# Linear attention and a gated feed-forward block on one core: the first batch's loads, the rule for PSUM banks and the order of group 0's output tiles

One NeuronCore of a Trainium2 chip runs the whole program. The metric is device time in microseconds (us), the median of several executions; all comparisons use executions in the fast state. "Span" is the time from the first to the last instruction of the one profiled execution, some 2 us less than the device time.

## The reference, cut

```python
B, H, S, D = 8, 8, 576, 64
def phi(x, c, s):
    r = np.maximum(x, 0.0)
    return np.concatenate([r * c, r * s], axis=-1)      # c, s: cos and sin of pi/2 * position / S
q_p, k_p = phi(q, cos_w, sin_w), phi(k, cos_w, sin_w)
kv  = np.einsum('bhsf,bhsd->bhfd', k_p, v)
num = np.einsum('bhsf,bhfd->bhsd', q_p, kv)
den = np.einsum('bhsf,bhf->bhs', q_p, np.sum(k_p, axis=2))[..., None] + 1e-06
x   = (num / den).transpose(0, 2, 1, 3).reshape(4608, 512)
out = (silu(x @ w_gate) * (x @ w_val)) @ w_out          # w_gate, w_val 512 x 1536, w_out 1536 x 512
```

## The kernel before

The 4608 rows go through the feed-forward part (FFN) in nine groups of 512. The attention of a batch is worked into the FFN of the group before it by a plan: `at(slot, step)` puts a step behind the products of a slot; a group has 16 slots. Loads with a cast (fp32 to bf16) are issued by GpSimd and share one queue; what needs no cast, the output writes and the DMA transposes ("turns") are issued by SyncE and share another.

```python
raw = ctx.enter_context(tc.tile_pool(name="raw", bufs=3))     # k, v, q of three batches at a time
...
def take(n, hold=None):                                       # PSUM banks in ring order, those held left out
    while True:
        b0 = (bank_at[0] + n - 1) // n * n % 8
        bank_at[0] = b0 + n
        if not any(b0 <= x < b0 + n for r in held.values() for x in r):
            break
...
def load(b, nm, parts=1):                                     # casting load, GpSimd
    ...
        nc.gpsimd.dma_start(out=t[:, sl].rearrange("p g c d -> p g (c d)"), in_=sv[:, sl])
def qturn_dma(b, e):                                          # turn of q by DMA, SyncE
    nc.sync.dma_start_transpose(out=qt_of(b)[:, e]..., in_=st[b, "q"][e * SH:(e + 1) * SH]...)
def qturn_pe(b, j, lo, hi, eng):                              # the same by PE and an engine that reads PSUM
    ...
def a_half(t, j):                                             # numerators of 128 rows: reads qt and kvd
    ...
for piece in range(3):                                        # group 0's output: four tiles side by side
    for t in range(OUT):
        ffn_out(t, 4 * piece, 4 * piece + 4)
        slot((piece, t))
for b in range(2, B):
    s0 = SLOTS * (b - 1)
    ...
        if b > 3:
            for s, nm in ((p0 - 2, "k"), (p0, "v"), (p0 + 2, "q")):
                at(s, lambda b=b, nm=nm: load(b, nm))         # waits until batch b-3 has left its buffers
    for e in range(2):
        at(tq[e], lambda b=b, e=e: qturn_dma(b, e))
```

## Time and profile before

| | before |
|---|---|
| device time | 339.96 us (339.66 to 344.24) |
| span | 337.0 us |
| PE busy | 97% of it |
| first FFN product | 18.23 us |
| first product of group 0's output | 45.11 us |
| first product of group 1 | 61.55 us |

The last three rows cut the span into an opening, group 0's FFN, group 0's output with batch 1's attention worked in, and the rest.

### The profile page before, as it was taken

How to read it: one execution, taken by the hardware profiler on the slowest of the kernel's cores; microseconds unless marked ns; L12 is line 12 of the kernel's file. 1: busy time of each engine (PE TensorE's matmuls, PEld its weight loads, DVE VectorE, ACT ScalarE, POOL GpSimd, SP SyncE). 2: the span in 40 equal slices, each digit the busy share in tenths (PEclk: the TensorE clock that was granted, in tenths of full speed). 3: DMA queues.
4: the chain of work that ended last, by engine and by line, in shares of the span. 5: the costliest groups of instructions: out<-in, count | busy, mean ns of one | idle time of the engine just before them, and what ended most of it. 6: DMA issues, size and time to landing. Idle time of an engine off the chain costs nothing.

```text
span 337.0 us, 5960 instructions
## 1 busy us (share of the span) xinstructions
PE 325.9 (97%) x2280; PEld 167.6 (50%) x2313; DVE 189.0 (56%) x424; ACT 158.0 (47%) x311; POOL 32.4 (10%) x50
## 2 busy tenths in 40 slices
PE   8889998999999999999999999999999999999995
PEld 3578854454444444444454444544454444444443
DVE  6664756389526952695259625971478138714420
ACT  6664456778326732673257415751354135413321
POOL 9454320011002000200000000000000000000000
PEclk9999999999999999999999999999999999999999
DMA  8999999999976828492810271017301410141013
GB/s 238 198 200 200 204 207 208 252 185 186 159 150 100 147 58 168 72 168 48 160 27 17 48 153 45 16 31 143 71 17 31 104 38 16 34 109 31 0 33 93
DMA packets 57084, 36.76 MB, mean 109 GB/s; under 512 B 31328, under 2 KB 52064, under 8 KB 57056
## 3 DMA queue, kind: packets, MB, share of 16 engines
q0 software_dynamic: 20624, 18.03, 33.8%
q1 hardware_dynamic: 36272, 18.23, 25.9%
q8 instruction: 18, 0.29, 0.3%
q10 hardware_dynamic: 160, 0.13, 0.1%
q14 instruction: 10, 0.08, 0.1%
HBM read 37.75 MB, written 9.44 MB: 140 GB/s over the span
## 4 chain that ended last, share of the span: by engine, by line
PE 93%; ACT 3%; DVE 2%; issue 1%; ACTq 0%
PE banks L377 53%; PE banks L403 27%; PE banks L316 5%; PE banks L132 3%; PE banks L237 3%; ACT sg L385 1%; DVE v L202 1%; DVE ht L387 1%; PE banks L357 1%; PE banks L421 0%; PE banks L285 0%; ACT xT L358 0%; PE banks L223 0%; ACT ob L410 0%; ACT qwT L277 0%
## 5 line engine op out<-in xcount | busy, mean ns | idle before, releaser
L377 PE MATMUL banks<-xT,wg_sb 128*128 128x512 bf16 (+2 forms) x474 | 112.4, 354 | 1.8 <-ACT xT L358 1.0
L387 DVE TENSOR_TENSOR ht<-sg,banks 128x512 bf16<-128x512 bf16 (+2 forms) x122 | 76.1, 624 | 66.4 <-PE banks L377 50.9
L377 PE MATMUL banks<-xT,wv_sb 128*128 128x512 bf16 (+2 forms) x479 | 111.7, 354 | 0.2
L385 ACT ACTIVATE sg<-banks 128x512 bf16<-128x512 f32 (+2 forms) x122 | 66.9, 548 | 90.3 <-PE banks L377 89.4
L403 PE MATMUL banks<-wo_sb,ht 128*128 128x512 bf16 x410 | 93.3, 379 | 0.6 <-issue 0.2
L377 PEld LDWEIGHTS <-wv_sb 128*128 128x128 bf16 x488 | 47.3, 98 | 46.3
L377 PEld LDWEIGHTS <-wg_sb 128*128 128x128 bf16 x488 | 45.8, 98 | 37.1 <-issue 2.2
L403 PEld LDWEIGHTS <-ht 128*128 128x128 bf16 x420 | 40.7, 98 | 46.1 <-issue 0.6
L410 DVE COPY ob<-banks 128x512 f32<-128x512 f32 x17 | 11.8, 692 | 56.3 <-PE banks L403 56.2
L326 ACT ACTIVATE tmp<-banks,cst 128x260 f32<-128x260 f32 x64 | 30.5, 477 | 13.6 <-PE banks L316 12.8
L410 ACT COPY ob<-banks 128x512 f32<-128x512 f32 x18 | 10.6, 587 | 55.9 <-PE banks L403 55.9
L327 DVE SCALAR_TENSOR_TENSOR num<-banks,cst,tmp 128x260 f32<-128x260 f32 x64 | 31.0, 485 | 7.1 <-ACT tmp L326 6.7
L316 PE MATMUL banks<-kvd,qt 128*128 128x260 bf16 (+1 forms) x144 | 24.9, 277 | 0.1
L341 DVE TENSOR_TENSOR x<-num,rec 128x256 bf16<-128x256 f32 x64 | 24.4, 422 | 1.1
L202 DVE TENSOR_TENSOR v<-raw_v,tab 128x1152 bf16<-128x1152 bf16 x30 | 22.3, 752 | 0.0
L316 PEld LDWEIGHTS <-qt 128*128 128x128 bf16 (+1 forms) x144 | 11.8, 100 | 16.0 <-issue 3.4
L188 ACT ACTIVATE raw_k<-raw_k 128x576 bf16<-128x576 bf16 x24 | 16.0, 675 | 0.0
L188 ACT ACTIVATE r_q<-raw_q 128x576 bf16<-128x576 bf16 x24 | 16.0, 675 | 0.0
L93 POOL DMA_DIRECT2D raw_k<-in_k_dram x9 | 7.0, 780 | 82.1 <-issue 78.9
L237 PE MATMUL banks<-v,raw_k 64*64 64x130 bf16 x576 | 11.9, 220 | 1.1 <-ACT kvd L249 0.9
L237 PEld LDWEIGHTS <-raw_k 64*64 64x64 bf16 x576 | 9.2, 106 | 7.0 <-issue 5.6
L132 PE MATMUL banks<-zeros 128*128 128x512 bf16 x37 | 11.1, 458 | 1.0 <-DVE zeros L127 1.0
(57 smaller groups left out, 113.0 us busy)
## 6 DMA issues: line engine op xcount, KB each, us to landing
out_dram<-ob SPq DMA_DIRECT2D x70, 128.0 KB, 2.4
raw_k<-in_k_dram POOLq DMA_DIRECT2D x7, 576.0 KB, 12.5
raw_v<-in_v_dram POOLq DMA_DIRECT2D x6, 576.0 KB, 13.6
raw_q<-in_q_dram POOLq DMA_DIRECT2D x6, 576.0 KB, 15.6
wg_sb<-in_moe_w_gate_dram POOLq DMA_DIRECT2D x6, 256.0 KB, 11.3
wv_sb<-in_moe_w_val_dram POOLq DMA_DIRECT2D x6, 256.0 KB, 11.3
wo_sb<-in_moe_w_out_dram POOLq DMA_DIRECT2D x3, 512.0 KB, 13.3
first_v<-in_v_dram SPq DMA_DIRECT2D x2, 576.0 KB, 4.2
```

The lines of the kernel that those rows point to most:

```text
L188: nc.scalar.activation(out=out, in_=in_, func=AF.Relu)
L202: nc.vector.tensor_tensor(out=v2s[b % 2][:, g, :, :, 0:D], in0=(first if b == 0 and g < 2 else {"v": raw_of(b, "v")})["v"][:, g].unsqueeze ...
L237: nc.tensor.matmul(out=ps[i * D:(i + 1) * D, e, j * 2 * D1:(j + 1) * 2 * D1], lhsT=raws[b, "k"][es, g, c], rhs=v2s[b % 2][es, g, c, :, 0:D ...
L316: nc.tensor.matmul(out=ps[ms, e, 0:4 * D1], lhsT=st[b, "qt"][:, e, j, c:c + n].rearrange("p c s -> p (c s)"), rhs=kvd[b % 2][:, e, j].rear ...
L326: nc.scalar.activation(out=tmp, in_=av[:, :, 0], func=AF.Copy, scale=cst[:, c0, 0:1])
L327: nc.vector.scalar_tensor_tensor(out=st["num", t][:, j], in0=av[:, :, 1], scalar=cst[:, c0, 1:2], in1=tmp, op0=ALU.mult, op1=ALU.add,)
L341: nc.vector.tensor_tensor(out=x[:, 4 * j * D:(4 * j + 4) * D].rearrange("p (i e d) -> p e i d", i=2, e=2), in0=num[:, hs, 0:D].rearrange(" ...
L377: nc.tensor.matmul(out=o, lhsT=w[:, kc, fs], rhs=xT[tg][:, kc, ts], start=(kc == 0), stop=(kc == KC - 1))
L385: nc.scalar.activation(out=sg[:, 0:n], in_=ps[0], func=AF.Silu)
L387: nc.vector.tensor_tensor(out=ht[:, fc, r:r + n], in0=sg[:, 0:n], in1=ps[1], op=ALU.mult)
L403: nc.tensor.matmul(out=o_ps[t], lhsT=ht[:, fc, r:r + P], rhs=wo_sb[:, fc], start=(fc == 0), stop=(fc == FC - 1))
L410: (nc.scalar.copy if t % 2 == 0 else nc.vector.tensor_copy)(out=ob, in_=ps)
```

## The change

Its intent has two parts. **The opening:** k and q of the first batch come in fp32 by SyncE's queue, which needs no cast; they are put where w_out and the second half of ht will stand later. q is turned first and multiplied by cos and sin afterwards, so 16 transposes do for 32. GpSimd's first weight load waits for v's second quarter (a small copy). **Group 0's output:** a bank is given by longest out of use and not in ring order, and the output tiles are worked by pairs, so two banks are held and not four.

```diff
     def take(n, hold=None):
-        while True:
-            b0 = (bank_at[0] + n - 1) // n * n % 8
-            bank_at[0] = b0 + n
-            if not any(b0 <= x < b0 + n for r in held.values() for x in r):
-                break
+        free = [b for b in range(0, 8, n) if not any(b <= x < b + n for r in held.values() for x in r)]
+        b0 = min(free, key=lambda b: sorted(used[b:b + n], reverse=True))
...
+    for gs in (slice(0, 1), slice(1, 2), slice(2, 4)):
         load_first("v", gs)
-    load_first("q", slice(0, G), slice(0, CUT[0]))
...
-    load(0, "k", 2)
-    load_slots(0, "q", CUT[0], NC)
+    load_first("k", slice(0, 1))
+    load_first("k", slice(1, 2))
+    load_first("q", slice(0, G), 0, 2)
+    load_first("k", slice(2, 3))
+    load_first("k", slice(3, 4))
+    load_first("q", slice(0, G), 2, 4)
...
+    hold = consts.tile([P, 1], FP32)
+    nc.gpsimd.tensor_copy(out=hold, in_=first["v"][:, 1, 0, 0:1])
+    load_w(0)
+    load_slots(0, "q", CUT[0], NC)
...
+    def weight_q(t):
+        for w in range(2):
+            nc.vector.tensor_tensor(out=qwT[t % 2][:, w]..., in0=qr[t % 2]..., in1=tabq[:, w, 2 * t:2 * t + 2]..., op=ALU.mult)
...
-    for piece in range(3):
-        for t in range(OUT):
-            ffn_out(t, 4 * piece, 4 * piece + 4)
-            slot((piece, t))
+    steps0 = [(piece, t) for piece in range(3) for t in range(2)] + [(piece, t) for t in (2, 3) for piece in range(3)]
+    for i, (piece, t) in enumerate(steps0):
+        ffn_out(t, 4 * piece, 4 * piece + 4)
+        slot(divmod(i, 4))
```

Cut: the opening's new order of steps (relu of k, kv, turns, first FFN products), the layout of xT, ht in two tiles. After group 0 the program is the same.

## The prediction

> **What bounds the kernel now.** I read the page first, then PE's waits over the whole span, then the chain in order of time, then the timeline of the first 30 us and of 36 to 62 us.
>
> ```profile
> PE 325.9 (97%) x2280; PEld 167.6 (50%) x2313; DVE 189.0 (56%) x424; ACT 158.0 (47%) x311; POOL 32.4 (10%) x50
> ```
>
> TensorE is the bound, and no other engine is near it. But busy time counts overlapping ends and the products on zeros (L132), so I ask where PE does no useful work. The waits of PE are few:
>
> ```profile
> PE banks L357 <- ACT ob L410: 1.3, 2, 0.7
> PE banks L132 <- DVE zeros L127: 1.0, 1, 1.0
> PE banks L377 <- ACT xT L358: 1.0, 2, 0.7
> PE banks L237 <- ACT kvd L249: 0.9, 1, 0.9
> PE banks L285 <- ACT qwT L277: 0.7, 1, 0.7
> PE banks L223 <- DVE num L327: 0.3, 1, 0.3
> ```
>
> All lie before 61 us: the same view from 62 us on is empty. Three are in the opening's chain (kvd, qwT, xT). Two are bank waits at the end of group 0 (L357 and L223 get a PSUM bank that another engine has only now stopped reading).
>
> **After 61.3 us nothing is to be had.** In the chain 16 products of 512 columns take 3.45 us, so 0.2156 us each. Eight groups of 144 make 248.4 us; 28 tiles of numerators at two times 0.22 us, with three tiles split between batches, 12.9; twelve kv halves of 0.65 us 7.8. Sum 269.1 us. PE's last product ends at 332.2, 270.9 us after 61.3, so at most 1.8 us are lost there. The 4.8 us tail (two ACT copies, output DMA) is untouched.
>
> **Before 61.3 us** I count useful PE work the same way: group 0's FFN products 96 x 4 x 0.0547 = 21.0 and 48 x 0.2156 = 10.4; transposes of weighted q 32 x 0.058 = 1.9; kv of two batches 2.6; a_tile 32 x 0.058 = 1.9; turns of x 1.8; turns of raw q 1.2; numerators 2.0. Sum 42.8 us. So some 17.5 us go to filler and waits: 8.6 before the first useful product, 5.7 from 9.4 to 24.6 us (15.2 us of time, 9.5 of work), about 1 from there to 45.1, and 2.5 from 45.1 to 61.3 (16.2 of time, 13.7 of work). The opening's chain:
>
> ```profile
> 0.99 8.61 PE banks L132 x28
> ...
> 10.08 0.72 PE banks L237 x35
> ...
> 12.67 0.85 PE banks L237 x36
> ...
> 14.49 0.48 PE banks L285 x8
> ...
> 17.75 0.64 PE banks L285 x8
> 18.39 0.91 PE banks L377 x16
> ```
>
> The first FFN product begins at about 18.2 us, and PE is filled with FFN from 24.6 us on. The two clean bank waits in the timeline:
>
> ```profile
> 57.69 0.38 PE L357 MATMUL banks<-ident,x 128*128 128x128 bf16 x4 [0.68 <-ACT ob L410]
> ...
> 60.47 0.38 PE L357 MATMUL banks<-ident,x 128*128 128x128 bf16 x4 [0.67 <-ACT ob L410]
> ```
>
> Each costs about 0.8 us of start-to-start time against an unbroken stream (the products before end their slots at 56.85 and 59.64).
>
> The arrivals of the first batch, from what began when its data landed:
>
> ```profile
> 8.34 1.71 ACT L265 ACTIVATE qw<-first_q,csk 128x256 bf16<-128x256 f32 x4 [1.11 <-DMA first_q<-in_q_dram]
> ...
> 11.01 0.46 DVE L190 TENSOR_SCALAR raw_k<-raw_k 128x1152 bf16<-128x1152 bf16 x1 [0.50 <-DMA raw_k<-in_k_dram]
> ...
> 18.82 0.74 POOL L176 DMA_DIRECT2D wg_sb<-in_moe_w_gate_dram  x1 [1.16 <-DMA wv_sb<-in_moe_w_val_dram]
> ```
>
> v landed at 4.5 and 6.0 us, the first slots of q at 8.3, k at 9.6 and 11.0. The POOL queue's waits tell when weights land: the first pair of weight slices at 15.6, the second at 18.8, the third at 21.2.
>
> **What the Trainium skill says.** "TensorE: Matmul & The Clock Gate", Part 1, gives N/2.4 GHz plus 2.5 ns for a warm product, half speed until PE has been busy for about 3.4 us, and a floor near 25 ns. The trace agrees on the first: 0.2156 us for 512 columns. The zero products' weight loads are 0.43 us apart until 6.0 us, half that after, so the slow phase was 5 us here. "DMA: Bandwidth & Descriptors", Queues, rings and completion order, says each engine goes round the queues packet by packet. Here q's first slots (0.52 MB) needed 2.36 us beside the casting k load, 222 GB/s, where v ahead of it ran at about 390. "VectorE: DVE Perf Modes", The perf-mode tier table, bears on the new products of turned q: 16-bit operands at two elements a cycle. The trace has 1152 such outputs in 0.75 us (L202), against 1.36 us from fp32. "ScalarE: Activation LUTs", What ACT_TABLE_LOAD costs, has 1283 ns a load; so has the trace, twice, and the change keeps both loads.
>
> **The change, part by part.**
>
> *First batch by the uncast queue.* In fp32 k is 1.18 MB, and q's first four slots 0.52, so 2.88 MB with v instead of 1.70. By the trace data runs from about 2.2 us at 390 GB/s and is seen 0.8 us after it has moved. Alone the queue would finish at about 10.4 us. But the weights start once v's second quarter is there (4.5 us), and in the trace a POOL load takes two us or so to move bytes, so from 6.5 us they share. Estimates: v at 3.8, 4.5 and 6.0; k's first half by 7.6; q's two slots at 8.5 to 9; k's last quarter at 10.7 with 270 GB/s for this queue or 11.6 with 222, say 11.1. That is no earlier than now. The gain must come from what follows.
>
> *q weighted after turning.* 32 transposes become 16 (the last two tiles use pairs of halves, which run side by side like L223): 0.9 us less PE. Two zero products per half of kv give back 0.4. Per tile: ACT now has four scaled relus or so and copies of 0.5 to 0.6, then one relu of 0.59; DVE has two products of about 0.4 each (512 outputs, from 0.75 for 1152).
>
> *The opening in order.* kv_first(0) starts when ACT has cast three quarters of v (5.3 to 7.2) and relu'd two of k (to 8.6). Filler ends near 8.2 to 9.3, depending on whether a 64-column zero product takes 30 or 56 ns, so I put the first useful product at 8.7, against 9.4. The last k lands at 11.1, its relus end at 11.5, kv_first(1) ends at 12.4, kvd is copied at 13.0 and a_tile(0) ends at 13.3, against 14.97. Denominator, reciprocal, two halves of x (0.17 + 0.20 + 0.42 + 0.42), turns and two parallel copies: xT is whole near 15.5, and FFN starts there, not at 18.2.
>
> From there DVE's order decides: each tile needs 1.06 for x, 0.8 for the weighting, 0.57 for two ht. a_tile(1) at 16.8, a_tile(2) at 20.0 (the second pair of weights, needed at 17.6, still lands at about 18.5, and PE waits in a gap that it had anyway), a_tile(3) at 23.1, full flow at 23.6. By then the same FFN work is done as now at 24.6 (64 short products against 32 short and 16 long, both 3.5 us), but one turn of x more remains (0.2). Gain: **0.8 us**. FFN starting 2.7 us earlier is mostly spent again in waits for DVE.
>
> *Banks and output tiles by pairs.* Before, four output banks are held through all of group 0's output, and ring order hands the turns of x a bank just left. Now two are held, and the longest unused one is given. Of the 2.5 us lost from 45.1 to 61.3 the two ob waits (1.6) should go, and the wait for num with the load after it (0.4): **2.0 us**. After 61.3: 0.2 of the 1.8, as PE's waits list nothing there.
>
> *Others.* The new layout of xT only cuts the moving operand into runs of 128, and the split ht changes addresses: 0.
>
> Sum: 0.8 + 2.0 + 0.2 = 3.0 us, and 0.5 for the fewer transposes and freer order of FFN halves behind the opening, where about 1 us was lost: 3.5 us. 339.96 - 3.5 = **336.5 us**.
>
> **Rivals.** (1) *The weights' transfers hold up k and q.* If sharing begins earlier or takes more than half, the last k lands at 12.5 and the opening gains nothing or loses 0.5: about 337.8. For it speaks 222 GB/s in the shared stretch; against it, that the weights' packets are shorter than k's, so a turn by packets favours k. (2) *The opening gains in full.* If DVE keeps up, PE's work from a_tile(0) on is some 6.7 us, so full flow could come at 20.5: 3 us more, about 333.5. Against it speaks DVE's sum of about 8 us over the same stretch. (3) *The clock.* Short zero products may fail to hold or win the full clock; the opening's products then take twice as long, costing 1 to 2 us: about 338. (4) *The bank wait is replaced.* With ob read later or x late on DVE, the turns of x wait for x itself; then the last stretch gains 0.8 and not 2.0: 337.7.
>
> **Range and chances.** The two gains are independent: the opening from -0.5 to +3, the banks from 0.8 to 2.4. That gives 334.3 to 338.8 for eight in ten. 2% is 6.8 us: it needs both in full and most of the first filler too, so 0.05. Slower by 2% would need a stall in every group, which the emptiness of PE's later waits makes unlikely: 0.01.
>
> **What would show it.** Right: no wait of PE for ob in group 0's output, that stretch near 14 us; first FFN product at 15 to 16 us; a_tile waits put down to DVE's weighting; after group 0 the same length to within 0.5 us. Wrong: k's last relu after 12 us (rival 1); weight loads of zero products 0.43 us apart beyond 6.5 us (rival 3); full FFN flow before 22 us (rival 2); any PE wait for banks after 62 us.

## More of the kernel before

Batch 2's q is the first that is turned by DMA and not by PE.

The prediction shows the waits of PE. Here are lines that it does not show, and that matter later. First the SyncE timeline of the kernel before, from 60 us (start, length, engine, operation): the turn of batch 2's q.

```profile
66.11 6.83 SPq L214 DMA_TRANSPOSE qt<-r_q  x2
```

Then GpSimd's timeline: the three casting loads of batch 5, issued once batch 2's buffers are free.

```profile
53.95 0.74 POOL L93 DMA_DIRECT2D raw_q<-in_q_dram  x1 [7.14 <-PE banks L223]
74.97 0.76 POOL L93 DMA_DIRECT2D raw_k<-in_k_dram  x1 [20.28 <-issue]
75.72 0.75 POOL L93 DMA_DIRECT2D raw_v<-in_v_dram  x1
76.45 0.76 POOL L93 DMA_DIRECT2D raw_q<-in_q_dram  x1
```

And the weight-load side of PE, where the first uses of that turned q stand, one for each of the two turns. The bracket is idle time and what ended it.

```profile
77.11 0.10 PEld L316 LDWEIGHTS <-qt 128*128 128x128 bf16 x1
77.42 0.10 PEld L316 LDWEIGHTS <-qt 128*128 128x128 bf16 x1 [0.21 <-DMA qt<-r_q]
```

The turned q comes just in time: the second turn is 0.21 us late for its weight load, and not at all late for PE's products, so that the view of PE's waits is empty here. The table by stage says how full the queues are at that time (the last two columns are the DMA engines' share, over 1 when several packets of an engine overlap in the record, and GB/s).

```profile
68.00:72.00 4.00, 3.95 (x52) 2.04 (x52) 4.00 (x7) 3.17 (x6) 0.00 (x0) 1.00 1.21 209
72.00:76.00 4.00, 3.95 (x52) 2.04 (x52) 3.12 (x7) 2.80 (x6) 1.03 (x2) 1.00 1.36 152
76.00:80.00 4.00, 4.00 (x22) 1.95 (x21) 3.90 (x10) 3.59 (x8) 1.21 (x2) 1.00 1.13 167
80.00:84.00 4.00, 4.00 (x22) 1.98 (x21) 3.90 (x11) 3.18 (x7) 0.00 (x0) 1.00 1.20 200
```

## The result

| | before | after |
|---|---|---|
| device time, median | 339.81 us (338.96 to 344.24) | 351.35 us (350.7 to 351.77) |
| span | 337.0 | 348.6 |
| first FFN product | 18.23 | 15.50 |
| first product of group 0's output | 45.11 | 45.61 |
| first product of group 1 | 61.55 | 60.01 |
| from there to the end | 275.5 | 288.6 |

The changed kernel is **slower**: ratio 1.0347, 95% interval 1.0318 to 1.0375. A ratio here is the mean time of one kernel's fast runs over that of the other's of the same rounds, so not quite the ratio of the medians quoted. (The run of 344.24 is more than 1.5% above the fastest, so it counts as slow and is left out of the ratio.)

The waits of PE, all of them, in the changed kernel (total us, times, longest):

```profile
PE banks L375 <- DMA qt<-r_q: 10.9, 2, 7.4
PE banks L296 <- ACT raw_k L214: 1.5, 2, 1.2
PE banks L440 <- DMA wv_sb<-in_moe_w_val_dram: 1.4, 2, 0.9
PE banks L149 <- DVE zeros L144: 1.0, 1, 1.0
PE banks L440 <- DMA wg_sb<-in_moe_w_gate_dram: 0.9, 1, 0.9
```

The waits for ob and num are gone, as intended. In their place stands one that the kernel before did not have: PE waits 10.9 us for batch 2's turned q. PE's timeline puts it in group 1:

```profile
79.40 0.28 PE L375 MATMUL banks<-kvd,qt 128*128 128x260 bf16 x1 [3.47 <-DMA qt<-r_q]
...
87.09 0.40 PE L375 MATMUL banks<-kvd,qt 128*128 128x260 bf16 x1 [7.41 <-DMA qt<-r_q]
```

SyncE's timeline and GpSimd's, to be laid beside those of before: the turn is issued 1.5 us earlier, batch 5's loads 1.8 to 2.2 us earlier.

```profile
64.56 9.71 SPq L243 DMA_TRANSPOSE qt<-r_q  x2
```

```profile
72.73 0.74 POOL L99 DMA_DIRECT2D raw_k<-in_k_dram  x1 [17.91 <-issue]
73.89 0.74 POOL L99 DMA_DIRECT2D raw_v<-in_v_dram  x1 [0.42 <-DVE v L231]
74.62 0.75 POOL L99 DMA_DIRECT2D raw_q<-in_q_dram  x1
```

The chain in order of time from 64 us (start, length, what):

```profile
66.90 20.14 DMA qt<-r_q
87.05 0.05 issue
87.09 0.40 PE banks L375
87.49 3.35 PE banks L440 x8
90.84 0.22 PE banks L375 x2
91.06 1.08 PE banks L440 x5
```

The second turn took 20.14 us from issue to landing, against 10.2 at most before. Eight products after it take 3.35 us, 0.42 each; the next five 0.216 each. So PE's clock had fallen to half while it idled (the trace's clock record has it at half from 80.4 to 90.6 us). The table by stage shows that in its third column from the right (1.00, then 0.55, 0.50, 0.67), and that DMA moves little meanwhile:

```profile
72.00:76.00 4.00, 3.93 (x30) 1.68 (x18) 3.55 (x10) 3.75 (x8) 2.22 (x3) 1.00 1.31 168
76.00:80.00 4.00, 0.28 (x1) 0.10 (x1) 2.45 (x4) 0.34 (x1) 0.00 (x0) 1.00 1.37 74
80.00:84.00 4.00, 0.00 (x0) 0.00 (x0) 0.00 (x0) 0.00 (x0) 0.00 (x0) 0.55 1.52 72
84.00:88.00 4.00, 0.91 (x3) 0.43 (x4) 0.00 (x0) 0.47 (x1) 0.00 (x0) 0.50 1.25 144
88.00:92.00 4.00, 4.00 (x15) 1.59 (x14) 1.51 (x3) 1.65 (x4) 0.00 (x0) 0.67 1.14 187
```

The sum of the spans' difference, 11.6 us: the opening with group 0's FFN +0.5; group 0's output -2.0 (14.40 in place of 16.44); the two waits +10.9; half clock after them some +1.8 (8 x (0.419 - 0.216) and three smaller products); about 0.4 is not assigned.

**What moved in those queues.** The trace has a record for every DMA packet. A casting load of k, v or q goes in packets of 1152 B, a turn in 256 B (2304 for the two of a batch), an output write in 2048 B. Counted per us of the span's time:

```
                                      casts per us    turn packets per us
casts alone                                ~180               -
casts and the turn together                ~140             ~143
turn, second half (before, 75.2 to 76.8)   under 25          ~690
                        first turn packet   the 2304th   casts beside it
before                        70.1              76.8     61, 27, 3 and 21 in the four us from 73 on
after                         68.5              85.2     16 at the least, never dry
```

Beside casts the turn gets about one packet for each of theirs. At 143 a us its 2304 packets need 16.1 us; after the casts have run dry, 3 us or less for the rest. How fast a turn is with no casts in the queues stands later in the kernel before: a half (1152 packets) issued at 94.65 us or later has its first packet some 1.2 us after the issue and lands after 3.7 to 4.0 us. Batch 2's two halves landed after 10.2 and 9.4 us before, and after 14.8 and 20.1 in the changed kernel.

Before, batch 4's casts ran dry around 75 us, and batch 5's came to move some 2 us after their issue at 74.97. In the changed kernel batch 5's were issued at 72.73 and followed batch 4's without a pause, and 68.5 + 16.1 is 84.6, near the 85.2 of the 2304th packet. But that fit is partly luck. The pace is not even: from 75 to 85 us the casts crawl there (16 to 64 packets a us), and the turn has two faster us (near 300), five at 122 to 162, and 30 to 44 at the end. And the turn of x, issued at 75.94 in the same queue, uses packets of the same size: some of its own may be counted, and the turn of q is seen to land only at 87.05.

### The profile page after: what moved, and what is told of

Its sections match the earlier page's. It is cut to its first block, busy times and chain, and to the rows that moved or that the text cites. A ratio compares the mean times of both kernels' runs of the same rounds, so it can differ in the third digit from the quotient of the medians.

```text
span 348.6 us, 6072 instructions
## 1 busy us (share of the span) xinstructions
PE 328.5 (94%) x2352; PEld 167.2 (48%) x2352; DVE 189.7 (54%) x422; ACT 156.4 (45%) x304; POOL 31.5 (9%) x49
## 3 DMA queue, kind: packets, MB, share of 16 engines
HBM read 37.75 MB, written 9.44 MB: 135 GB/s over the span
## 4 chain that ended last, share of the span: by engine, by line
PE 85%; DMA 10%; ACT 2%; POOL 1%; issue 0%; DVE 0%; ACTq 0%; SPq 0%
PE banks L440 50%; PE banks L467 26%; DMA qt<-r_q 6%; PE banks L375 4%; DMA wv_sb<-in_moe_w_val_dram 3%; PE banks L266 2%; DMA wo_sb<-in_v_dram 1%; ACT r_q L214 1%; ACT sg L448 1%; PE banks L486 0%; PE banks L252 0%; POOL wg_sb L202 0%; PE banks L422 0%; ACT raw_k L214 0%; PE banks L342 0%
## 5 line engine op out<-in xcount | busy, mean ns | idle before, releaser
L440 PE MATMUL banks<-xT,wv_sb 128*128 128x512 bf16 (+2 forms) x496 | 114.5, 353 | 1.4 <-DMA wv_sb<-in_moe_w_val_dram 1.4
L440 PE MATMUL banks<-xT,wg_sb 128*128 128x512 bf16 (+2 forms) x496 | 114.9, 354 | 0.9 <-DMA wg_sb<-in_moe_w_gate_dram 0.9
L385 ACT ACTIVATE tmp<-banks,cs_all 128x260 f32<-128x260 f32 x64 | 30.5, 477 | 25.2 <-PE banks L375 24.4
L386 DVE SCALAR_TENSOR_TENSOR num<-banks,cs_all,tmp 128x260 f32<-128x260 f32 x64 | 31.0, 484 | 15.9 <-ACT tmp L385 15.5
L375 PE MATMUL banks<-kvd,qt 128*128 128x260 bf16 (+1 forms) x144 | 25.2, 278 | 10.9 <-DMA qt<-r_q 10.9
L375 PEld LDWEIGHTS <-qt 128*128 128x128 bf16 (+1 forms) x144 | 11.8, 100 | 27.6 <-DMA qt<-r_q 11.6
L231 DVE TENSOR_TENSOR v<-raw_v,tab 128x1152 bf16<-128x1152 bf16 x31 | 23.1, 753 | 2.2 <-ACT raw_v L497 2.2
L99 POOL DMA_DIRECT2D raw_k<-in_k_dram x7 | 5.2, 742 | 95.0 <-issue 57.2
L266 PEld LDWEIGHTS <-raw_k 64*64 64x64 bf16 x504 | 7.8, 106 | 5.6 <-issue 4.7
L266 PE MATMUL banks<-v,raw_k 64*64 64x130 bf16 x504 | 10.2, 220 | 0.0
L149 PE MATMUL banks<-zeros 128*128 128x64 bf16 (+1 forms) x64 | 9.0, 302 | 1.0 <-DVE zeros L144 1.0
## 6 DMA issues: line engine op xcount, KB each, us to landing
wo_sb<-in_moe_w_out_dram POOLq DMA_DIRECT2D x3, 512.0 KB, 13.1
```

The source lines that it names most:

```text
L231: nc.vector.tensor_tensor(out=v2s[b % 2][:, g, :, :, 0:D], in0=(first if b == 0 and g == 0 else {"v": raw_of(b, "v")})["v"][:, g].unsqueez ...
L266: nc.tensor.matmul(out=ps[i * D:(i + 1) * D, e, j * 2 * D1:(j + 1) * 2 * D1], lhsT=raws[b, "k"][es, g, c], rhs=v2s[b % 2][es, g, c, :, 0:D ...
L375: nc.tensor.matmul(out=ps[ms, e, 0:4 * D1], lhsT=st[b, "qt"][:, e, j, c:c + n].rearrange("p c s -> p (c s)"), rhs=kvd[b % 2][:, e, j].rear ...
L385: nc.scalar.activation(out=tmp, in_=av[:, :, 0], func=AF.Copy, scale=cst[:, c0, 0:1])
L386: nc.vector.scalar_tensor_tensor(out=st["num", t][:, j], in0=av[:, :, 1], scalar=cst[:, c0, 1:2], in1=tmp, op0=ALU.mult, op1=ALU.add,)
L440: nc.tensor.matmul(out=o, lhsT=w[:, kc, fs], rhs=xT[tg][:, ts, kc], start=(kc == 0), stop=(kc == KC - 1))
```

## The experiments

**Theory A.** The turn of batch 2's q was just in time before. The change moves PE's need of it 1.5 us earlier, moves the casts ahead of it later, and moves batch 5's loads earlier, so that the pause in which the turn finished is gone. **Theory B.** Something in the changed kernel itself slows the turn: its places in memory, its order on SyncE. **Theory C.** The clock, or chance.

All runs, in the order of the argument. "Output" is the start of group 0's first output product in the run's profile, "rest" the span from there to the end, "wait" PE's total wait for the turned q. The medians of e1 and e13 leave out one slow run each; e1b and e8 are single runs, whose state is unknown.

| run | what | median us | ratio to before [95%] | output | rest | wait |
|---|---|---|---|---|---|---|
| before | | 338.9 (profiled) | | 45.11 | 291.9 | 0 |
| e16_before_again | before, unchanged | 339.23 | 1.0011 [0.9979, 1.0043] | 45.54 | 292.0 | 0 |
| after | the change | 351.35 | 1.0347 [1.0318, 1.0375] | 45.61 | 303.0 | 10.9 |
| e3_pe_turn | after, batch 2's q by PE | 339.65 | 0.9965 [0.9888, 1.0042] | 48.12 | 291.3 | 0 |
| e1_hold_loads | after, batch 5's loads held | 342.06 | 1.0026 [0.9938, 1.0115] | slow profile | | |
| e1b_hold_again | the same, one look | 343.31 | | 45.39 | 295.8 | 3.8 |
| e2_idle_3us | after, 3 us of useless work | 341.48 | 1.0024 [0.9937, 1.0112] | 45.41 | 294.5 | 1.3 |
| e11_before_4_buffers_mended | before, loads earlier | 352.88 | 1.0408 [1.0363, 1.0454] | 45.77 | 304.9 | 10.3 |
| e7_opening_only | the opening alone | 343.28 | 1.0084 [1.0023, 1.0145] | 45.58 | 296.6 | 2.3 |
| e4_banks_pairs_only | banks and pairs alone | 340.83 | 0.9967 [0.9869, 1.0065] | 49.47 | 289.9 | 0 |
| e4b_banks_pairs_again | the same again | 342.01 | 1.0062 [1.0036, 1.0088] | 45.50 | 295.2 | 3.3 |
| e8_banks_only | bank rule alone, one look | 338.98 | | 46.63 | 290.5 | 0 |
| e8b_banks_only | the same | 340.6 | 1.0033 [0.9994, 1.0073] | 48.35 | 290.5 | 0 |
| e14_banks_pairs_hold | banks, pairs, loads held | 341.04 | 1.0056 [1.0021, 1.0091] | 47.88 | 289.9 | 0 |
| e6_banks_pairs_pe_turn | banks, pairs, q by PE | 339.36 | 0.9969 [0.9918, 1.002] | 47.94 | 291.6 | 0 |
| e12_banks_pairs_early_turn | banks, pairs, turn early | 340.82 | 1.0034 [0.9996, 1.0072] | 45.57 | 294.5 | 2.6 |
| e13_after_early_turn | after, turn early | 348.48 | 1.0227 [1.0176, 1.0277] | 46.97 | 299.4 | 7.2 |
| e15_after_turn_act_queue | the same, by another queue | 344.09 | 1.0136 [1.0101, 1.0171] | 44.79 | 296.9 | 0 |
| e10_no_first_hold | e3 without the first hold | 340.97 | 1.005 [1.0014, 1.0085] | 48.38 | 291.2 | 0 |

e5_before_4_buffers gave a wrong result; see below. All others are correct.

### Is it the turn? e3

The changed kernel, but batch 2's q is turned by PE from PSUM, with no DMA:

```diff
         if b == 2:
-            steps = steps[G:] + steps[:G]
+            turns = [lambda j=j, lo=lo, hi=hi: qturn_pe(2, j, lo, hi, "act") for j in range(J) for lo, hi in ((0, 5), (5, NC))]
+            steps = turns + steps[:G]
...
-        for e in range(2):
+        for e in range(2 if b > 2 else 0):
             at(tq[e], lambda b=b, e=e: qturn_dma(b, e))
```

> The changed kernel with batch 2's q turned by PE (as batch 1's is) and not by the DMA transpose; 36 more transposes on PE, about 1.0 us. Both theories: the wait for qt of batch 2 is gone, 351.3 - 13 + 1 = about 339.3 us. If another wait (x turned by DMA, or batch 3's q) takes its place, over 343 us; this says how much of the loss hangs on these two transposes alone.

339.65 us, level with before; no wait for q is left. So all of the loss hangs on that one wait.

### Is it batch 5's loads? e1, e1b, e2

A small GpSimd copy from the turned q stands ahead of batch 5's loads, so that they can't be issued before it has landed:

```diff
+            if b == 5:
+                def hold_pool():
+                    hold2 = consts.tile([P, 2], BF16, name="hold2")
+                    nc.gpsimd.tensor_copy(out=hold2, in_=st[2, "qt"][:, :, 0, 0, 0])
+                at(34, hold_pool)
```

> The changed kernel, but GpSimd may not issue batch 5's k, v and q loads until both DMA transposes of batch 2's q have landed (a two-element copy that reads their result stands ahead of the loads). Theory A (the transposes crawl because casting loads stay queued beside them without a pause: batch 5's loads come right behind batch 4's): the wait of PE for qt falls from 10.9 us to under 3, the landing from 20 us to under 13, the time from 351.3 to about 340.5 us. Theory B (something of the changed kernel itself makes the transposes slow: the new place of tiles in memory, the new layout of xT, the new order of output writes ahead of them in the same queue): nothing changes, 349 to 353 us.

342.06 us in the median of its three fast runs, ratio 1.0026: nine of the eleven us are back.

> The changed kernel with batch 5's loads held, once more, because its first profile fell in the slow state. Theory A: a wait for qt under 3 us, transposes of batch 2's q landing in under 13 us, 340.5 to 342.5 us.

```profile
PE banks L375 <- DMA qt<-r_q: 3.8, 2, 2.9
```

The wait is 3.8 and not 10.9, the longer of the two landings 14.2 us and not 20.1; both a little over what I had expected. The rest that remains I put down to batch 4's own casts beside the turn, until these run dry. So batch 5's loads make the greater part of the stall, and a smaller part is there without them.

The other way to test "PE is early": 3 us of useless products (14 on zeros) at the start of group 1.

```diff
+        if tg == 1:
+            idle_products(14)
         for fc in range(FC):
             ffn_fc(tg, fc)
```

> The changed kernel with 14 useless products on zeros (3.0 us of PE) ahead of group 1, so that its transposes, its batch 5 loads and the moment when turned q is needed all come 3 us later against the same loads of batch 4. Theory A (it is a matter of when batch 4's loads are done against batch 5's issue): the wait vanishes and the kernel is faster with the useless work than without: 351.3 + 3.0 - 13 = about 341 us. Theory B (slow transposes as such): 354 us.

341.48 us, some 10 us faster than the changed kernel **with more work in it**. Batch 5's loads are issued at 75.55 there, the turn lands in 10.7 us, and the wait falls to this:

```profile
PE banks L375 <- DMA qt<-r_q: 1.3, 1, 1.3
```

### Does the kernel before get it too? e5, e11

Theory B says that the changed kernel has it in itself. So I gave the kernel before a fourth buffer for raw k and v, which lets batch 5's k and v be issued earlier, and nothing else of the change. To make room, v's fp32 copy goes where w_out will stand.

```diff
-                raws[b, nm] = raw.tile(...)
+                raws[b, nm] = (raw if nm == "q" else raw4).tile(...)     # raw4: bufs=4
...
-    first = {}
+    wo_sb = consts.tile([P, FC, d_model], BF16)
+    first = {"v": wo_sb...bitcast(FP32)...}
```

> The kernel before with a fourth buffer each for raw k and raw v (and v's first batch lying in w_out's place, to make room). Nothing else is changed: the opening, the banks, the transposes, the layout of xT are those of before. With a fourth buffer batch 5's k and v loads need not wait for kv_mm of batch 2 and are issued right behind batch 4's q, at about 55 us and not at 75. Theory A (the transposes of batch 2's q crawl for as long as casting loads are queued beside them): the kernel before gets the stall too, a wait of PE for qt of 5 us or more, 345 to 352 us, although more buffers never make anything wait in themselves. Theory B (the changed kernel's own memory places, layout or order): no stall, 339 to 341 us.

The first form was my mistake: the weight loads stood ahead of the products that read v in the same place; v's readers waited 36 us, and the result was wrong. Its 379 us say nothing. Mended, v's products stand ahead of the weight loads:

> The run with a fourth buffer for raw k and v again, mended: in the first, w_out's loads stood ahead of the products that read v in the same place, so v waited 36 us and was overwritten (its time says nothing). Now v's products are put ahead of the weights' loads in the program, as in the changed kernel. Theory A: batch 5's k and v are issued at about 55 us, casting loads are queued without a pause, and the kernel before gets a wait of PE for qt of 5 us or more: 345 to 352 us. Theory B: no stall, 339 to 341 us.

Its GpSimd timeline, its SyncE timeline and PE's waits:

```profile
55.79 0.76 POOL L94 DMA_DIRECT2D raw_k<-in_k_dram  x1 [0.44 <-DVE x L343]
56.54 0.75 POOL L94 DMA_DIRECT2D raw_v<-in_v_dram  x1
67.04 0.74 POOL L94 DMA_DIRECT2D raw_q<-in_q_dram  x1 [9.75 <-ACT r_q L190]
```

```profile
66.77 10.22 SPq L216 DMA_TRANSPOSE qt<-r_q  x2
```

```profile
PE banks L318 <- DMA qt<-r_q: 10.3, 2, 7.7
```

The kernel before has the whole stall, 10.3 us against 10.9, with nothing of the change in it. Theory B falls. (The edit also moves v's place and puts v's products earlier in the program; group 1 starts at 62.21 against 61.55, so PE's need is not earlier.) The packets are the cleanest here: the turn moves 134 a us with casts beside it all the time, 2304 from 70.7 to 88.0 us. Apart from one us, from 79 to 80, neither kind crawls in this run, so the uneven pace named above isn't needed for the stall.

### Which part brings it? e7, e4, e4b, e8, e8b

The opening alone is the changed kernel with the old bank rule and the old order of output tiles (the last hunk of the change and the one in `take` undone):

> The changed kernel with the old bank rule and the old order of group 0's output pieces: the opening alone. By the traces the opening makes FFN reach the same point 0.5 us later than before and POOL's loads about 2 us later. Theory A: the transposes are needed at about the time of before, batch 4's loads end about 1.5 us later, batch 5's come as in before: a wait for qt of 1 to 6 us, 341 to 347 us, clearly less than the whole change's 351. Theory B with the cause in the opening (memory places, layout of xT): the whole stall, 351 us or more.

343.28 us; PE waits 2.3 us. The opening delays the casts: the first load of w_out is issued at 29.28 us in the changed kernel, at 27.07 before. Group 0's output takes 16.43 us, as before.

Banks and pairs alone are the kernel before with those two hunks:

> The kernel before with only the bank rule and the output tiles of group 0 by pairs. Group 1 then starts 2 us earlier while the opening and its loads are as before. Theory A: the transposes' margin (0.2 us of wait in the kernel before) is gone and batch 5's loads come 2 us earlier, so a wait for qt of 3 us or more appears: 342 to 350 us in spite of the 2 us won. Theory B with the cause in the opening's memory places or in xT's layout: no wait, 338.0 us. Theory B with the cause in the order of the output writes: a wait as in the changed kernel, but then the run that holds the loads must not help.

340.83 us, and in its profile no wait for q at all: I had expected one of 3 us or more. But there the opening was late (the first slots of q landed at 10.4 us and not at 8.3, and the clock fell), so that everything after it stood 4.4 us later, and so did PE's need. Six more runs of it, beside six of an unchanged copy of the kernel before:

> The kernel before with bank rule and pairs alone, again, beside the unchanged kernel in the same call. Group 0's output stretch is 14.4 us again (2.0 under before). If the opening's arrivals are the same by chance as in the kernel before, the mean is 1 to 2 us under it, 337 to 338.5. If something in the new rule delays the opening or the turn of q eats the gain (landing over 9.5 us with a wait of PE), it is level with it, 338.5 to 341.

> The kernel before, unchanged, once more, as a measure of chance. In its one profile the first slots of q were there at 8.3 us; in six profiles of kernels with the new bank rule and the very same loads they came at 8.6 to 10.4 and PE waited up to 2.3 us for them. If that arrival is chance, this profile has it anywhere between 8.3 and 10.5, the ratio is 1.000 within 0.003, and some of the six runs are at 340 to 342. If the kernel before is always early, it is at 8.3 to 8.7 and five or six of six runs are under 339.5.

```profile
PE banks L323 <- DMA qt<-r_q: 3.3, 2, 2.2
```

With the opening on time the expected wait is there, 3.3 us, and the kernel is slower than before, 1.0062 [1.0036, 1.0088]. So the 2.0 us won in group 0's output are lost again in group 1, and more. (Not PE alone is earlier: batch 5's loads are issued at 73.31, 1.7 us earlier than in the kernel before.) The unchanged copy gives 1.0011 [0.9979, 1.0043], so chance is about 0.3% here, a tenth of the loss; Theory C falls.

The bank rule alone:

> The kernel before with the bank rule alone, output tiles four at a time as before. From the first product of group 0's output to the first of group 1 the kernel before took 16.4 us and every kernel with both parts 14.4. With the bank rule alone: about 15 us if the bank handed out too soon was the greater part, 16 us if four held output banks leave it no choice.

> The kernel before with only the new bank rule, again, now with rounds (one look gave 338.98). Group 0's output stretch there was 15.0 us (46.63 to 61.64 in that run), against 16.4 before and 14.4 with the pairs as well: so 1.4 us gained if nothing else moves, 338.2 to 338.9 in runs with a clean opening. If the 0.7 us step of PE also costs the turn of q its slack (it was just in time), a wait for qt of 1 to 2 us shows and the time is that of before.

Group 0's output takes 15.01 us in both: of the 2.0 us the bank rule gives 1.4 and the pairs 0.6. The total doesn't show it (338.98 once, then 340.6): in both profiles the first slots of q landed at 10.0 to 10.4 us. With the same loads they landed at 8.3 in both profiles of the kernel before and at 8.6 to 10.4 in seven with the new bank rule. Nothing in the rule touches those transfers. Two things speak for chance: e11, with the old rule, has these slots only at 9.2, and with the changed opening the last k is taken up at 11.85 us in one profile and 14.82 in another. The kernel before also has fast runs of 341.6 to 343.2 us at a granted clock of 0.988 to 0.993 (six in the calls of e1 and e5), but none of them was profiled. So whether it is chance in these seven stays open.

### Can the gain be kept? e14, e6, e12

Banks and pairs with batch 5's loads held as in e1:

> The kernel before with the new bank rule and the pairs, and with batch 5's three casting loads held on GpSimd until the turned q of batch 2 has landed (a small copy from it, ahead of them). If those loads behind batch 4's are what slows the turn, PE waits for qt under 1.5 us in the profile in every run, and the time is that of the clean runs of banks and pairs, 338.0 to 338.6, so 1.3 us or so under the kernel before; runs with a clock drop in the opening are 341 or so. If the hold only moves the contention to batch 5's own use, PE waits for k or v of batch 5 later (after 150 us) and the time is at 340 or above.

No wait for q, and 289.9 us from the first output product to the end, exactly 2.0 under the kernel before. But the opening was late again (q at 9.99 us), and the median is 341.04. Since a late opening by itself gives the turn its time (e4 has the same 289.9 without the hold), this run does not show that the hold is what helps.

Banks and pairs with q turned by PE:

> The kernel before with the bank rule, output tiles by pairs, and batch 2's q turned by PE (so that the stall can't come). 2.0 us won at the end of group 0, 1.0 us of PE given for 36 transposes: theory A 338.3 us in undisturbed runs against 339.3 of the kernel before; if turned q still holds up the turns of x or batch 3, 340 or more.

339.36 us: no wait, but PE's own work for the turn eats 1.7 us of the 2.0 (291.6 against 289.9).

Banks and pairs with the relu of q and its turn put into group 0's output, issued at 62.10 us:

> The kernel before with the bank rule, the pairs, and batch 2's relus of q and DMA transposes some 5 us earlier (relus in group 0's last output pieces, transposes ahead of group 1). Nothing is taken from the transposes' work or from the loads. Theory A: crawling at one packet of 256 bytes for each casting packet, 144 a us, the 2304 packets need some 16 us, so from about 60 us on they end at about 76, when they are needed: a wait for qt under 2 us, 337.5 to 338.5 us in undisturbed runs against 339.3, the best so far. If the wait stays at 3 us or more, the pace next to the loads is not what holds them.

340.82 us and still a wait of 2.6 us: the turn only stands longer beside batch 4's casts.

### Would an earlier turn have saved the change? e13, e15

The same in the changed kernel, issued at 63.49 us:

> The changed kernel with only that: batch 2's relus of q and DMA transposes some 5 us earlier. Theory A: the wait for qt falls from 10.9 to under 3 us, 338.5 to 341 us. Theory B (transposes slow in themselves in this kernel): at most the 5 us come off, 346 us.

The wait is 7.2 us; I had expected under 3. Its first packet moves at 67.7 us, and I put this down to group 0's output writes, which stand ahead of it in SyncE's queue. So I issued it from ScalarE, which has a queue of its own, at 59.74 us:

```diff
     def qturn_dma(b, e):
-        nc.sync.dma_start_transpose(
+        (nc.scalar if b == 2 else nc.sync).dma_start_transpose(
```

> The changed kernel, with the turn of batch 2's q issued early (as in the run before that moved it to 63.5 us and still waited 7.2 us) and from the ScalarE queue, so that group 0's output writes no longer stand ahead of it. If standing behind the writes is why the early issue bought so little, the first transpose packet now moves within 3 us of the issue, the two are done before batch 5's loads move, and PE waits for qt under 2 us: 340 to 342. If the turn beside any casts is slow by itself (one for one), about 2304 packets at 143 a us take 16 us from 63.5: landing near 80 and a wait of 1 to 4 us: 342 to 345.

That explanation falls. The first packet moves 4.0 us after the issue here too (3.8 to 4.2 in the fifteen correct profiles with this turn on SyncE), with nothing ahead of it in that queue; I put the delay down to the casts, since with none in the queues it was 1.2 us. Then the turn goes one for one beside the casts until they thin out near 76, and lands at 79.5 us, near the second expectation's 80. And the issue itself holds ScalarE, whose silu PE then waits for:

```profile
59.74 10.81 ACTq L243 DMA_TRANSPOSE qt<-r_q  x2
70.65 1.57 ACT L448 ACTIVATE sg<-banks 128x512 bf16<-128x512 f32 x3 [10.94 <-issue]
```

```profile
PE banks L440 <- ACT sg L448: 5.0, 1, 5.0
```

344.09 us. An early issue doesn't help while the casts run; the turn needs a pause in them, or PE.

### Where is the opening's gain? e10

The changed kernel with q turned by PE, and without the copy that holds the weights' loads until v's second quarter is there:

```diff
-    hold = consts.tile([P, 1], FP32)
-    nc.gpsimd.tensor_copy(out=hold, in_=first["v"][:, 1, 0, 0:1])
```

> The changed kernel with batch 2's q turned by PE (no stall, as in the run that did this alone), and without the GpSimd copy that holds the weights back until v's second quarter is there. If that copy is why the second pair of weights landed at 20.5 and not at 18.5, the second pair lands before 19 here, PE's wait for wv_sb (0.9) goes, and the first output product of group 0 comes 0.5 to 1 us earlier than 45.6; time 338.5 to 339.5. If sharing the bandwidth is the cause, the last k lands later than 11.9 and the opening is no shorter: 339.5 to 341.

```profile
PE banks L296 <- ACT raw_k L214: 2.8, 2, 2.3
PE banks L320 <- DVE qf L312: 1.5, 1, 1.5
```

The weights' wait is gone, but k and q come later: the last k is taken up at 14.85 us (11.85 in the changed kernel), and the first FFN product is at 19.75, not 15.50. I would put that down to bandwidth shared with the weights, were it not that e3, which has the hold, was as late in its profile (14.82 and 19.50), and has v late too. In six other profiles with the hold the first FFN product is at 14.8 to 15.8 us. So this is inconclusive: the run doesn't show that the hold costs anything, and the gain that I hoped for (338.5 to 339.5) isn't there at 340.97.

## Why the prediction was wrong

1. **The step that failed** is "After 61.3 us nothing is to be had", with its two uses: "after group 0 the same length to within 0.5 us", and slower by 2% "would need a stall in every group, which the emptiness of PE's later waits makes unlikely". The later part became 13.1 us longer, by a stall in one group alone. An empty list of waits says that nothing was late, not by how much it was early. Batch 2's turned q had no slack at all: the weight load waited 0.21 us for it, in a view that I had not read. e11 shows that the kernel before stalls as much when its loads come earlier; e4b that PE stalls 3.3 us when group 1, and with it PE's need and batch 5's loads, comes 1.7 us earlier; e7 that it waits 2.3 when batch 4's casts come later. The change does all of this, and the waits are not the sum of e4b's and e7's, 5.6, but 10.9: with both, the pause between batch 4's and batch 5's casts, in which the turn had finished, is gone.
2. **"No wait for ob, that stretch near 14 us"** was right: 14.40, a gain of 2.04 against 2.0. By parts it is 1.4 for the bank rule and 0.6 for the pairs.
3. **The opening.** The first FFN product at 15.50 is what I predicted (15.5). The gain of 0.8 by the first output product did not come: 45.61 against 45.11 and 45.54 in two profiles of before. One term was mis-sized: the second pair of weights was to land at 18.5 and landed when the wait for wv_sb at 20.48 us ended. PE's timeline:

```profile
15.50 0.52 PE L440 MATMUL banks<-xT,wg_sb 128*128 128x128 bf16 x4
16.47 0.40 PE L440 MATMUL banks<-xT,wv_sb 128*128 128x128 bf16 x4 [0.45 <-DMA wv_sb<-in_moe_w_val_dram]
...
20.48 0.40 PE L440 MATMUL banks<-xT,wv_sb 128*128 128x128 bf16 x4 [0.93 <-DMA wv_sb<-in_moe_w_val_dram]
```

   The last k was there at 11.85, not at 11.1. The prediction also let the weights move two us after their issue, from 6.5 us on; their first packet came at 9.34, 4.2 us after the issue at 5.18. Its own trace had that delay: the first packet of the casting k came at 6.50, 4.1 us after the issue at 2.37. The same packets say that the 222 GB/s for q were no rate beside casts: up to 6.5 us its queue moved 330 to 360 GB/s with no cast packet beside it. That the late start made the second pair late fits, but no run isolates it. And the sum of lost time before 61.3 us is 18.5 us (61.3 - 42.8), not 17.5, as the first useful product stands at 9.44 and not 8.6; no forecast hangs on it. With loads alike, other profiles of this opening have the first output product at 44.79 to 48.12 us, so a difference of half a us can't be settled by single profiles.
4. **The 0.2 and 0.5 us.** The 0.2 for the steady part is not there: e4, e8, e8b and e14 have the new bank rule and no stall, and take 275.5 us from group 1's first product to the end, as before. The 0.5 for "the fewer transposes" can't be told from the spread in point 3.
5. **The rivals.** Rival 1 (the weights' transfers) came in a weak form. Rival 4 (the bank wait is replaced) was the nearest in kind: a wait did take the place of the one removed, but I sought it in the same stretch, at 1.2 us, and it stood 20 us later at 10.9. Rival 3's slow clock came after the stall, not in the opening's zero products: 1.8 us.
6. **Still open:** why casts and turn both crawl for part of 75 to 85 us in the changed kernel; and whether the later arrival of the first q under the new bank rule is chance. No version beats the kernel before: of those run in rounds the best two, e6 and e3, are level with it.

## What to carry to other kernels

Before moving an engine earlier, look up what it consumes next from a DMA, and how long before its use that landed: a transfer that is just in time shows no wait, and takes back every us that is won ahead of it. Loads of later data that wait only for a free buffer are issued earlier too, and can take the bandwidth from the transfer that is needed first; a small copy that holds them back, or even a few us of useless work, can be worth ten. Read the waits of the weight loads and the issue-to-landing times beside the waits of PE.

## What the Trainium skill lacked or had wrong

- "Advanced Engine Details and Errata", X-Bar Transpose (TRN2), says that transposing DMAs are as fast as regular ones, with 350 to 400 GB/s to be expected. Here a half of a turn (1152 packets of 256 B) with no casts beside it took 2.0 to 2.3 us from its first to its last packet in the kernel before, some 130 to 150 GB/s, and batch 2's second half, once the casts thinned out, some 690 packets a us, 178 GB/s; beside casting loads it was some 143 a us, 37 GB/s: a turn of 0.59 MB then takes 16 to 17 us. The page doesn't give the cost beside another stream.
- "DMA: Bandwidth & Descriptors", Issuing engines are not separate DMA queues, calls the time on the sequencer usually small. Issuing the two turns held ScalarE for 10.81 us in e15, and 6.83 to 10.22 us of SyncE's time in the others shown; PE lost 5.0 us by it in e15.
- No page says how the delay from the issue of a transposing DMA to its first packet grows beside casting loads: some 1.2 us with none in the queues of the kernel before, 3.8 to 4.2 us beside them for batch 2's turn in sixteen profiles.
- No page has the stretch in the changed kernel in which casting loads fell to 16 to 64 packets a us and the turn beside them at last to 30 to 44, where each had some 140 a few us earlier.
